# Score tiles of 64 by 32, a first batch in pieces, TensorE in source order and two earlier loads in a fused attention and WaveMLP kernel

## The chip, the cores and the metric

The kernel runs on one core of a Trainium2 chip. The metric is the device time of one execution in microseconds (us); lower is better. A time is the median of several executions, with the lowest and highest in brackets. A profile has its own span, about 2 us shorter than the device time of the same execution (172.6 us beside 174.73 us for the kernel before).

A ratio is the mean time of one kernel's fast runs over the mean time of the other's fast runs of the same rounds, with a 95% interval. It is therefore not quite the ratio of the medians that are quoted.

## The reference

```python
# B=4 batches, H=8 heads, S=768 tokens, D=64; window 96, 8 global keys
scores = q @ k.T / sqrt(64) - slope[h] * dist        # masked to window + global keys
x      = softmax(scores) @ v                         # -> (B, 768, 512)
theta  = x @ w_theta                                 # 512 x 512
y      = w_tok_r @ (x * cos(theta)) + w_tok_i @ (x * sin(theta))   # 768 x 768 token mixing
u      = x + y
out    = u + relu(u @ w_ch)                          # 512 x 512
```

## The kernel before

A batch passes through fixed stages: scores (TensorE), exponentials (ScalarE), values (TensorE), division into `x_sb` (VectorE), transposition to `xT`, `theta` (96 matmuls), sines (ScalarE), products `zri` (VectorE), mixing (288 matmuls of 512 columns in all four batches), `u`, `uT`, and the channel matmul `chan`. The attention of batch b+1 is woven into the mixing of batch b, so that TensorE has mixing to do while scores wait for exponentials. For batch 0 there is nothing to weave it into: its attention is a latency chain before the first mixing matmul. Batches are counted from 0.

In batch 0, and for q and k of batches 1 and 2, TensorE transposes. `xT` and `uT` of batches 1 to 3 (but for the very last token block), and q and k of batch 3, are transposed by DMA, issued one after another from SyncE (SP).

The local window needs, for each block of 128 keys, the block's own 128 queries and the next 128. Of the second half only 96 keys count, so the 8 global keys are overlaid there: VectorE makes `kG`, a copy of `kT` with global keys in it.

```python
def kglob(b, p):                      # VectorE: copy, then overlay the 8 global keys
    ...
    nc.vector.tensor_copy(out=kG, in_=kT[:, T:(NT - 1) * T].rearrange(...))
    nc.vector.tensor_copy(out=kG[:, :, 0:NG], in_=kT[:, None, 0:NG].to_broadcast(...))

def score_mms(b, p, c):               # weights 64 x 128, 128 columns, two heads on two row tiles
    ...
    for part in range(2 if jt + 1 < NT else 1):
        for hh in range(2):
            lhsT = kG[R, jt - 1, :] if part and jt else kT[R, own]
            nc.tensor.matmul(pb[:, hh, o:o + T], lhsT=lhsT, rhs=qT[R, (own, nxt)[part]], ...)

# batch 0 is written by hand inside `manual`, where engines keep source order
...
    trans_w(0, nc.scalar.copy); xtrans(0, NP - 1)
    for c in range(NT // 2):
        theta(0, c, 0); theta(0, c, 1)
manual.close()                        # from here the scheduler may reorder within an engine
```

The line numbers in the profiles are these:

| operation | before | after | e3 (before with the new tiles) |
|---|---|---|---|
| score matmuls / exponentials | L295 / L302 | L288 / L296 | L290 / L298 |
| values / `x_sb` | L352 / L362 | L343, batch 0 L363 / L349, L367 | L348 / L358 |
| theta / sines | L389 / L395 | L394 / L402 | L385 / L391 |
| mixing / chan | L409 / L434 | L425 / L450 | L405 / L430 |
| `kG` | L218, L220 | none | none |
| q,k cast `qkn` / its transposes | L229 / L244 | L223 / L238 | L224 / L239 |
| DMA transposes xT / uT / kT, qT | L366 / L423 / L262 | L377 / L439 / L255 | L362 / L419 / L257 |

The softmax here doesn't subtract the row's maximum and nothing guards it: scores larger than these inputs give would overflow.

## Time and profile before

The time before is 174.58 us (174.41 to 174.96). The page of the profile gives, per engine, busy time, share of the span and instructions, and per DMA queue its packets, megabytes and share:

```profile
span 172.6 us, 3652 instructions
PE 159.9 (93%) x1482; PEld 83.5 (48%) x1482; DVE 128.5 (74%) x288; ACT 99.1 (57%) x124; POOL 37.9 (22%) x45
...
q8 instruction: 11, 0.18, 0.4%
```

TensorE (PE) is the limit over the whole, but 93% busy does not say where the rest goes. The stage table does. I worked it out from the start times of TensorE's matmuls in the trace; "idle" is the time between starts less the work between them, at the spacing that this trace shows at full clock (216 ns for 512 columns, 56 ns for a transpose, 29 ns for a value matmul, and so on). Every matmul is charged its time at full clock, so the slowness of a cold clock is counted as idle too: in the kernel before 512 columns take 427 ns instead of 216 until 3.9 us. The work is 144.4 us.

| stage of before | from us | lasts us | of it idle us |
|---|---|---|---|
| first matmul to first theta | 1.2 | 26.8 | 11.1 |
| batch 0: theta to mixing | 28.0 | 5.2 | 0.0 |
| batch 0 mixing to batch 1 mixing | 33.16 | 47.20 | 6.3 |
| batch 1 mixing to batch 2 mixing | 80.36 | 33.90 | 3.1 |
| batch 2 mixing to batch 3 mixing | 114.26 | 33.57 | 2.7 |
| batch 3 mixing to last matmul | 147.83 | 20.82 | 0.1 |

The chain of waits (start us, duration us, what) shows the start as a chain through VectorE (DVE), with `kG` and `x_sb` in it:

```profile
7.78 1.01 DVE kG L218
8.81 0.18 DVE kG L220
...
26.33 0.56 DVE x_sb L362
...
28.15 3.45 PE pb L389 x16
31.60 1.53 PE ps L389 x7
33.16 2.84 ACT cs L395 x5
```

From 43 to 61 us VectorE is full. The busy table of that stretch (stretch, length, then PE, PEld, DVE, ACT, POOL busy with counts, PE clock, DMA, GB/s) has it at 17.94 of 18 us:

```profile
43.00:61.00 18.00, 17.20 (x228) 10.56 (x226) 17.94 (x41) 12.28 (x16) 5.74 (x7) 1.00 2.38 175
```

### The profile page before, as it was taken

What the parts mean: (1) busy time and instruction counts of PE and PEld (TensorE: products, weight loads), DVE (VectorE), ACT (ScalarE), POOL (GpSimd) and SP (SyncE); (2) the same over time, 40 slices, a digit from 0 to 9 for tenths busy, and PEclk for the clock granted to TensorE, in tenths of its full rate; (3) what the DMA queues carried; (4) which work ended last, traced back from release to release, by engine and by line L of the source; (5) the groups of instructions that cost most, each with busy time, mean ns of one, the idle gap of its engine ahead of it and who ended that gap; (6) DMA issues with size and microseconds to landing.
All of it is one profiled execution on the core that took longest, in us unless ns stands there. A gap on an engine that the chain in (4) does not pass through costs nothing.

```text
span 172.6 us, 3652 instructions
## 1 busy us (share of the span) xinstructions
PE 159.9 (93%) x1482; PEld 83.5 (48%) x1482; DVE 128.5 (74%) x288; ACT 99.1 (57%) x124; POOL 37.9 (22%) x45
## 2 busy tenths in 40 slices
PE   6479979999999999999999998999999989999991
PEld 1245655455756566544455463444554634444440
DVE  7678965678999999999587588597786837724443
ACT  2479676999497595489834740979348308500010
POOL 8974355005272010099300000000000000000000
PEclk9999999999999999999999999999999999999998
DMA  5999999999999999879999997787138571323335
GB/s 146 192 193 178 210 208 209 204 204 171 160 204 175 166 155 128 132 97 154 210 141 80 224 158 165 138 152 226 30 76 113 135 171 40 142 41 102 100 93 182
DMA packets 75088, 25.92 MB, mean 150 GB/s; under 512 B 63168, under 2 KB 72128, under 8 KB 75072
## 3 DMA queue, kind: packets, MB, share of 16 engines
q0 software_dynamic: 45680, 12.45, 78.4%
q1 hardware_dynamic: 28976, 12.72, 36.6%
q10 hardware_dynamic: 416, 0.52, 0.9%
q8 instruction: 11, 0.18, 0.4%
q14 instruction: 5, 0.04, 0.1%
HBM read 25.69 MB, written 6.29 MB: 185 GB/s over the span
## 4 chain that ended last, share of the span: by engine, by line
PE 59%; DVE 21%; ACT 10%; DMA 6%; issue 1%; SPq 0%; DVEq 0%; ACTq 0%
PE ps L409 29%; PE ps L434 10%; PE pb L389 5%; PE pb L295 4%; PE pb L352 4%; DVE x_sb L362 4%; ACT etab L142 3%; PE ps L389 3%; ACT e L302 3%; DMA qk<-in_k_dram 3%; DVE kG L218 2%; DVE e L312 2%; ACT cs L395 2%; DMA kT<-qk 2%; DMA xT<-x_sb 2%; PE ps L244 2%
## 5 line engine op out<-in xcount | busy, mean ns | idle before, releaser
L409 PE MATMUL ps<-zri,w_tokT 128*128 128x512 bf16 x288 | 70.6, 380 | 0.3 <-DVE o_sb L440 0.2
L302 ACT ACTIVATE e<-pb 128x1024 bf16<-128x1024 f32 (+1 forms) x48 | 43.6, 958 | 23.1 <-PE pb L295 22.9
L409 PEld LDWEIGHTS <-w_tokT 128*128 128x128 bf16 x288 | 26.1, 98 | 29.0 <-issue 1.0
L414 DVE TENSOR_TENSOR u<-x_sb,ps 128x512 bf16<-128x512 bf16 x24 | 16.4, 682 | 14.6 <-PE ps L409 14.6
L434 PE MATMUL ps<-w_ch_bf,uT 128*128 128x512 bf16 x96 | 24.2, 379 | 0.0
L398 DVE TENSOR_TENSOR zri<-x_sb,cs 128x512 bf16<-128x512 bf16 x48 | 17.9, 418 | 8.0 <-ACT cs L395 7.8
L440 DVE SCALAR_TENSOR_TENSOR o_sb<-ps,u 128x512 f32<-128x512 f32 (+1 forms) x25 | 16.5, 662 | 3.1 <-PE ps L434 3.1
L395 ACT ACTIVATE cs<-pb,halfpi 128x1024 bf16<-128x1024 f32 x8 | 8.9, 1116 | 15.7 <-PE pb L389 15.7
L312 DVE TENSOR_TENSOR e<-e,etab 128x1024 bf16<-128x1024 bf16 (+1 forms) x24 | 14.7, 615 | 3.4 <-ACT e L302 3.4
L389 PE MATMUL pb<-w_theta_bf,xT 128*128 128x512 bf16 x64 | 15.2, 379 | 1.0 <-DMA xT<-x_sb 1.0
L295 PE MATMUL pb<-qT,kT 64*128 64x128 bf16 x224 | 15.6, 219 | 0.6 <-DVE qT L211 0.3
L295 PEld LDWEIGHTS <-kT 64*128 64x128 bf16 x224 | 9.0, 94 | 14.1 <-issue 12.5
L389 PEld LDWEIGHTS <-xT 128*128 128x128 bf16 x96 | 9.0, 98 | 12.0 <-DMA xT<-x_sb 2.4
L428 ACT COPY uT<-ps 128x512 bf16<-128x512 bf16 x7 | 4.1, 587 | 18.6 <-PE ps L427 18.6
L352 PEld LDWEIGHTS <-e 128*128 128x128 bf16 x352 | 12.7, 97 | 3.3 <-issue 1.5
L434 PEld LDWEIGHTS <-uT 128*128 128x128 bf16 x96 | 8.9, 98 | 10.0 <-ACT uT L428 0.3
L295 PE MATMUL pb<-qT,kG 64*128 64x128 bf16 x128 | 11.7, 217 | 1.2 <-DVE kG L220 1.2
L88 POOL DMA_DIRECT2D vn<-in_v_dram x5 | 9.7, 1930 | 12.2 <-DVE vn L68 10.6
L362 DVE TENSOR_TENSOR x_sb<-pb,rec 128x768 bf16<-128x768 f32 x12 | 11.4, 949 | 0.3
L315 DVE TENSOR_TENSOR e<-e,etab 128x1024 bf16<-128x1024 bf16 x12 | 8.2, 684 | 2.8 <-ACT e L302 2.8
L352 PE MATMUL pb<-vn,e 128*128 128x65 bf16 x168 | 9.6, 193 | 0.3 <-DVE x_sb L362 0.3
L82 POOL DMA_DIRECT2D qk<-in_q_dram x8 | 7.4, 920 | 8.8 <-DVE qkn L229 5.0
(74 smaller groups left out, 203.0 us busy)
## 6 DMA issues: line engine op xcount, KB each, us to landing
out_dram<-o_sb SPq DMA_DIRECT2D x23, 256.0 KB, 2.4
vn<-in_v_dram POOLq DMA_DIRECT2D x3, 768.0 KB, 22.7
qk<-in_q_dram POOLq DMA_DIRECT2D x2, 768.0 KB, 21.0
qk<-in_k_dram POOLq DMA_DIRECT2D x2, 768.0 KB, 23.6
w_nat<-in_moe_w_tok_r_dram POOLq DMA_DIRECT2D x3, 384.0 KB, 13.7
w_nat<-in_moe_w_tok_i_dram POOLq DMA_DIRECT2D x3, 384.0 KB, 14.6
vn<-in_v_dram POOLq DMA_DIRECT2D x2, 384.0 KB, 8.9
qk<-in_q_dram POOLq DMA_DIRECT2D x8, 96.0 KB, 9.7
```

The lines of the kernel that those rows point to most:

```text
L295: nc.tensor.matmul(pb[:, hh, o:o + T], lhsT=lhsT, rhs=qT[R, (own, nxt)[part]], start=bool(b), stop=bool(b) or (jt == NT - 1 or (j == 1 and ...
L302: ins = nc.scalar.activation(e_c, pb[:, :, 0:n], AF.Exp, scale=scale).ins
L312: nc.vector.tensor_mul(e_c, e_c, tab[:, :, s0:s0 + n // T].rearrange("p a s n -> p a (s n)"))
L352: nc.tensor.matmul(o, lhsT=l_, rhs=r_, start=(i_ == 0), stop=(i_ == len(mms) - 1))
L362: nc.vector.tensor_mul(xv, po4[:, :, :, 0:D], rec.to_broadcast([T, n, NT, D]))
L389: nc.tensor.matmul(pb[j_] if last else pb[:, j_, :], lhsT=xT[:, dc, st(j_)], rhs=w_theta_bf[:, dc, :], start=(dc == 0), stop=(dc == NC - 1))
L395: nc.scalar.activation(o, p_, AF.Sin, **bias)
L398: nc.vector.tensor_mul(zri[b][:, i_, 2 * c + j_, :].rearrange("p (g d) -> p g d", g=NP), xb[:, :, 2 * c + j_, :], cs[:, i_, j_].rearrange( ...
L409: anchor["pe"] = nc.tensor.matmul(ps, lhsT=w_tokT[wi][:, st, tt * T:(tt + 1) * T], rhs=zri[b][:, wi, st, :], start=(st == 0 and wi == 0), ...
L414: anchor["dve"] = nc.vector.tensor_add(u_sb[b, tt].rearrange("p (g d) -> p g d", g=NP), x_sb[b][:, :, tt, :], ps.rearrange("p (g d) -> p g ...
L434: nc.tensor.matmul(ps_c, lhsT=uT[:, dc, :], rhs=w_ch_bf[:, dc, :], start=(dc == 0), stop=(dc == NC - 1))
L440: nc.vector.scalar_tensor_tensor(o_sb[:, cols], in0=ps_c[:, cols], scalar=0.0, in1=u[:, cols], op0=ALU.max, op1=ALU.add)
```

## The change

The intent is to shorten the start, to take `kG` off VectorE, and to save changes of tile mode. What such a change costs is in the trace of before: from a mixing matmul to the first score of a visit 311 ns pass (216 between two mixing matmuls), and from the last score to the next matmul of 512 columns 148 ns (a pair of scores takes 56), so 92 to 95 ns each way. Its parts:

1. Scores on tiles: weights of 64 x 32, mostly 256 columns, eight tiles at once. Only the first group of 32 keys needs the global keys, so a slice of `kT` serves and `kG` goes.
2. Batch 0 by pieces: values in 12 pieces, theta starting while values still run, the first two token blocks mixed in a hand-written order; warm-up matmuls 6 to 5.
3. TensorE keeps source order after batch 0 too (`ordered`).
4. q and k of batch 1 are loaded ahead of the last third of the token weights; the weaving starts earlier (0.3 to 0.1).

Smaller edits ride along: in batch 0 the first loads of q and k swap their queues, all eight `diag` tiles are made at the start, and one copy of token weights moves from ScalarE to VectorE.

```diff
+            if tt == NT - 2:                      # load_w: ahead of the last third of w_tok
+                load_all_qk(1)
-                for hh in range(2):               # score_mms
-                    lhsT = kG[R, jt - 1, :] if part and jt else kT[R, own]
-                    nc.tensor.matmul(pb[:, hh, o:o + T], lhsT=lhsT, rhs=qT[R, (own, nxt)[part]], ...)
+            for g in range(T // GS):              # GS = 32
+                parts = [(own, 0, 1), (slice(0, GS), 1, n)][:n] if g == 0 and jt else [(own, 0, n)]
+                for keys, a, z in parts:
+                    for hh in range(2):
+                        nc.tensor.matmul(pb[P, hh, (2*j+a)*T:(2*j+z)*T], lhsT=kT[R, keys],
+                                         rhs=qT[R, (jt+a)*T:(jt+z)*T], ...)
 ...
-    load_all_qk(1)
-    warm(6)
+    warm(5)
 ...
+    values0(2, 1)                                 # batch 0, the end of the hand-written order
+    values0(3, 1)
+    theta_mms(0, 0, 0)
+    xtrans0(1, dve)
+    theta_mms(0, 0, 1)
+    theta_sines(0, 0)
+    ...
+    theta_mms(0, 2, 0)
+    theta_mms(0, 2, 1)
+    theta_sines(0, 2)
+    mix(0, 0, 0)
 ...
+    ordered = ExitStack()
+    ordered.enter_context(tc.manual_schedule(engines={mybir.EngineType.PE}))
 ...
-        weave(main, side, 0.3 if b == 0 else 0.0, 0.9)
+        weave(main, side, 0.1 if b == 0 else 0.0, 0.9)
 ...
+    ordered.close()
```

## The prediction

> **What bounds it.** From 28 us to the end TensorE is the limit; the busy table gives it 93% of 172.6 us. From start-to-start times in its timeline (216 ns for 512 columns, 56 ns a transpose, 29 ns a value matmul, 28 ns a score matmul) I estimate 146 us of array work. The rest is array idle: about 12 us before 28 us, 6.5 us from 28 to 80, under 6 us after, 3.5 us of tail. The first 28 us are a latency chain: in the chain of waits VectorE is nearly unbroken from 6.8 to 25 us (kG, x_sb, qkn, qT, xT); the first mixing matmul (L409) starts at 33.2 us, held by the sines (L395), which start at 29.9. From 43 to 61 us VectorE is busy 17.9 of 18 us and ScalarE did the bias tables (L142) until 42.4, with q and k of batch 1 arriving near 41 us; the array loses 4.5 us there.
>
> **What changes.**
> 1. kG disappears: 16 copies of 0.39 us and 16 of 0.18 us, 9.1 us of VectorE; 2.4 us lie in the start chain, 4.6 us in the saturated stretch 43 to 80 us.
> 2. Scores: 352 matmuls of 64x128 weights by 128 columns become 896 of 64x32, mostly 256 columns. In the trace two row tiles start 3 to 4 ns apart and a pair takes 56 ns; [...]so eight should overlap too (the trace shows only two). Then a key block costs an estimated 110 ns against 112: no change. Entering and leaving the tile mode costs about 95 ns each way; the instruction order has 28 such visits against 38 (-1.9 us)[...]. Net near zero. [...]
> 3. First batch by pieces: values in 12 pieces, theta beginning while the last values run. ScalarE runs exponentials nearly back to back from about 9 to 23 us. I estimate the sines at 24.5 us, the first mixing at 27.5, the first two token blocks mixed near 33.5 instead of 39: 4 to 5.5 us.
> 4. q and k of batch 1 land near 32 us (two loads of token weights fewer ahead of them), so the saturated VectorE stretch begins earlier. This keeps the gain of 3 through batch 1; with kG gone it adds 1.5 us.
> 5. TensorE in source order: fewer mode changes, but no filling of waits, for example where three score visits run close together and wait for PSUM and exponentials: -1 to +1.5 us. After 80 us little changes.
>
> **Sum.** 174.6 - 5 (start) - 1.5 (VectorE stretch) + 0.5 (scores) + 0.4 (order) = 169.0 us. Range 164.5 to 174.5. Chances: faster 0.68, same 0.26, slower 0.06.
>
> **Signs.** Right: first mixing matmul at 26 to 29 us; batch 1's theta at about 67 us instead of 72; VectorE busy 7 to 9 us lower; score matmuls starting 3 to 6 ns apart, a pair of chunks lasting about 0.52 us. Wrong: score matmuls 25 ns apart or more; waits of scores for exponentials above 3 us in all; a longer time from batch 2's theta to the end.
>
> **What would break it.** [...]eight diagonals ahead of the first casts delaying the start[...]; stalls of the fixed order behind the bias tables; later token weights arriving too late for their transposes.

The sum came to 174.6 - 5 - 1.5 + 0.5 + 0.4 = 169.0 us. "Net near zero" and the +0.5 us for scores stand as my estimates. That eight tiles overlap as two do was my extrapolation from the trace of before.

## The result, and the profile after

The changed kernel takes 180.2 us (180.0 to 180.71, four runs); the kernel before took 174.77 us (174.41 to 176.08, four runs). The ratio is 1.0301 (1.0243 to 1.0359): slower by 3%. Executions over 1.5% slower than the fastest of the same kernel are left out of the means. The page after:

```profile
span 178.0 us, 4681 instructions
PE 159.0 (89%) x1996; PEld 85.4 (48%) x2025; DVE 125.3 (70%) x265; ACT 97.6 (55%) x119; POOL 37.9 (21%) x45
...
q8 instruction: 16, 0.26, 0.7%
```

There are 1,029 recorded instructions more (some matmuls have no record: 1,996 stand beside 2,025 weight loads), and queue q8, named "instruction", has moved 16 blocks of 16 KB instead of 11. The stages, worked out as before:

| stage | before us | after us | difference |
|---|---|---|---|
| first batch's mixing starts | 33.16 | 32.26 | -0.9 |
| batch 0 mixing to batch 1 mixing | 47.20 | 50.76 | +3.6 |
| batch 1 mixing to batch 3 mixing | 67.47 | 70.20 | +2.7 |
| batch 3 mixing to last matmul | 20.82 | 20.82 | 0 |

The gain at the start is 0.9 us, and two losses follow that have, as the experiments show, different causes. The start first. The chain of waits after:

```profile
25.51 1.08 PE pb L394 x5
...
27.64 0.42 DVE x_sb L367
28.19 0.43 DVE x_sb L367
28.67 0.28 PE ps L373 x2
29.01 1.03 PE pb L394 x4
30.03 0.67 PE ps L170 x12
30.70 1.73 PE pb L394 x8
32.43 0.86 PE ps L425 x4
```

`kG` is gone from the chain. In its place theta (L394) waits piece by piece for `x_sb` and the small transposes (L373). Then 12 transposes of token weights and the last 8 theta matmuls stand in the fixed order ahead of the first mixing matmul (L425). The first sines start at 26.6 us instead of 29.9, but the mixing does not start 3 us earlier, because all of theta is still ahead of it. Before the first mixing TensorE's array is idle for 10.4 us after and 11.1 us before, by the count of the stage table. These figures hide a cold clock: full clock came at 12.5 us instead of 3.9. With the matmuls ahead of it charged at the doubled time that they show (427 and 107 ns), the idle time is an estimated 6 us after and 9.7 before. So the pieces did remove waits, while cold matmuls took about 3 us more; e1 shows how much of that an earlier clock gives back.

Next, the stretch from the first mixing to batch 1's. In the chain of waits after:

```profile
48.34 0.86 PE ps L425 x4
49.20 0.39 PE pb L288 x16
49.62 3.57 ACT e L296 x4
53.23 0.37 PE pb L288 x12
...
64.21 1.73 ACT e L296 x2
```

For 3.57 us the chain runs through four exponentials on ScalarE. TensorE's timeline shows three groups of scores there, each behind a wait for an exponential, 1.32 us together:

```profile
51.61 0.41 PE L288 MATMUL pb<-qT,kT 64*32 64x256 bf16 x18 [0.54 <-ACT e L296]
52.31 0.42 PE L288 MATMUL pb<-qT,kT 64*32 64x128 bf16 x20 [0.29 <-ACT e L296]
53.23 0.37 PE L288 MATMUL pb<-qT,kT 64*32 64x128 bf16 x18 [0.49 <-ACT e L296]
```

In the kernel before the scheduler had put mixing between such groups:

```profile
51.77 0.61 PE L409 MATMUL ps<-zri,w_tokT 128*128 128x512 bf16 x2
...
52.63 0.60 PE L409 MATMUL ps<-zri,w_tokT 128*128 128x512 bf16 x2
```

The busy table of the whole stretch agrees; TensorE falls from 17.20 to 14.30 us while VectorE is still nearly full:

```profile
43.00:61.00 18.00, 14.30 (x314) 9.52 (x323) 17.43 (x31) 12.10 (x15) 6.95 (x8) 1.00 2.21 179
```

The tiles themselves work. The timeline of TensorE shows a visit of four key blocks after as one group of 38 matmuls:

```profile
83.98 0.63 PE L288 MATMUL pb<-qT,kT 64*32 64x256 bf16 x38
```

Inside it the trace has starts 3 to 4 ns apart on eight tiles (83.976, 83.980, 83.983, ...) and a new key block every 112 ns (84.096, 84.208, 84.320). So the array time of scores is what was predicted.

Last, q and k of batch 1. They land at 31.5 and 35.3 us instead of 37.4 and 41.3. VectorE's timeline shows when their first cast (L223) starts after, which is 40.77 us:

```profile
38.32 0.69 DVE L430 TENSOR_TENSOR u<-x_sb,ps 128x512 bf16<-128x512 bf16 x1 [0.95 <-PE ps L425]
39.18 0.69 DVE L430 TENSOR_TENSOR u<-x_sb,ps 128x512 bf16<-128x512 bf16 x1 [0.17 <-PE ps L425]
39.78 1.01 DVE L171 COPY w_tokT<-ps 128x768 bf16<-128x768 bf16 x2
40.77 0.43 DVE L223 COPY qkn<-qk 128x768 bf16<-128x768 bf16 x1
```

And before, which is 41.28 us:

```profile
41.28 1.16 DVE L229 COPY qkn<-qk 128x768 bf16<-128x768 bf16 x4
```

The data came 6 us earlier and the work began 0.5 us earlier. In VectorE's queue the casts stand behind `u` of token blocks 0 and 1 (38.32 and 39.18 us), which in the new order finish together and late.

### The profile page after: what moved, and what is told of

The parts are those of the page before. It is cut to its first block, busy times and chain, and to the rows that moved or that the text cites. A ratio compares the mean times of both kernels' runs of the same rounds, so it can differ in the third digit from the quotient of the medians.

```text
span 178.0 us, 4681 instructions
## 1 busy us (share of the span) xinstructions
PE 159.0 (89%) x1996; PEld 85.4 (48%) x2025; DVE 125.3 (70%) x265; ACT 97.6 (55%) x119; POOL 37.9 (21%) x45
## 4 chain that ended last, share of the span: by engine, by line
PE 72%; ACT 12%; DVE 8%; DMA 3%; issue 3%; POOL 0%; DVEq 0%; POOLq 0%
PE ps L425 31%; PE ps L450 11%; PE pb L394 7%; ACT e L296 7%; PE pb L288 6%; PE pb L343 4%; DMA xT<-x_sb 3%; PE pb L268 3%; PE ps L238 3%; PE ps L394 2%; PE ps L206 2%; ACT cs L402 1%; PE ps L170 1%; DVE x_sb L367 1%; PE ps L363 1%
## 5 line engine op out<-in xcount | busy, mean ns | idle before, releaser
L425 PE MATMUL ps<-zri,w_tokT 128*128 128x512 bf16 x269 | 65.9, 379 | 2.7 <-issue 1.3
L425 PEld LDWEIGHTS <-w_tokT 128*128 128x128 bf16 x288 | 26.3, 98 | 31.0 <-DVE w_tokT L171 1.8
L430 DVE TENSOR_TENSOR u<-x_sb,ps 128x512 bf16<-128x512 bf16 x24 | 16.4, 685 | 12.5 <-PE ps L425 12.5
L450 PE MATMUL ps<-w_ch_bf,uT 128*128 128x512 bf16 x91 | 23.3, 379 | 0.4 <-issue 0.2
L288 PE MATMUL pb<-qT,kT 64*32 64x256 bf16 (+1 forms) x896 | 17.8, 257 | 5.1 <-ACT e L296 2.3
L402 ACT ACTIVATE cs<-pb,halfpi 128x1024 bf16<-128x1024 f32 x9 | 10.0, 1115 | 20.6 <-PE pb L394 19.8
L394 PE MATMUL pb<-w_theta_bf,xT 128*128 128x512 bf16 x70 | 17.1, 379 | 2.7 <-DMA xT<-x_sb 2.6
L288 PEld LDWEIGHTS <-kT 64*32 64x32 bf16 x896 | 10.8, 92 | 17.8 <-issue 14.3
L394 PEld LDWEIGHTS <-xT 128*128 128x128 bf16 x96 | 8.8, 98 | 13.3 <-DMA xT<-x_sb 4.1
L343 PEld LDWEIGHTS <-e 128*128 128x128 bf16 x264 | 9.6, 97 | 3.3 <-issue 1.1
L245 ACT COPY kT<-ps 128x768 bf16<-128x768 bf16 x8 | 6.4, 799 | 7.9 <-PE ps L238 7.9
L402 ACT ACTIVATE cs<-pb 128x1024 bf16<-128x1024 f32 x9 | 9.2, 1022 | 0.0
```

The source lines that it names most:

```text
L288: nc.tensor.matmul(pb[P, hh, (2 * j + a) * T:(2 * j + z) * T], lhsT=kT[R, keys], rhs=qT[R, (jt + a) * T:(jt + z) * T], start=bool(b), stop ...
L343: nc.tensor.matmul(o, lhsT=l_, rhs=r_, start=(i_ == 0), stop=(i_ == len(mms) - 1))
L394: nc.tensor.matmul(pb[j_] if last else pb[:, j_, :], lhsT=xT_sb[b][:, dc, st(j_)], rhs=w_theta_bf[:, dc, :], start=(dc == 0), stop=(dc == ...
L402: nc.scalar.activation(o, p_, AF.Sin, **bias)
L425: anchor["pe"] = nc.tensor.matmul(ps, lhsT=w_tokT[wi][:, st, tt * T:(tt + 1) * T], rhs=zri[b][:, wi, st, :], start=(st == 0 and wi == 0), ...
L430: anchor["dve"] = nc.vector.tensor_add(u_sb[b, tt].rearrange("p (g d) -> p g d", g=NP), x_sb[b][:, :, tt, :], ps.rearrange("p (g d) -> p g ...
```

## The experiments

Sixteen kernels were run; all gave correct results. Times are medians; "before" is always the kernel before in the same rounds. The theory at the outset was that the fixed order causes the loss. The rivals were the tiles (by their own waits, or by the longer instruction stream), a cold clock, and the loads.

### e1: more warm-up matmuls in the changed kernel

```diff
-    warm(5)
+    warm(8)
```

> The changed kernel with 8 idle matmuls at the start instead of 5. Cold-clock theory: with 5 of them the TensorE clock was raised only at 12.5 us (before: 3.9 us with 6), and about 7 us of the start chain are TensorE pieces at half speed; with 8 the clock comes up near 4 us and the kernel gains 1.5 to 3 us (about 177.5 to 178.5 us in the chip's time), first mixing matmul near 30.5 us instead of 32.4. Rival (VectorE chain limits the start): clock comes up early, but under 0.7 us is gained, about 179.7.

Measured: 179.31 us (178.68 to 179.91), ratio to before 1.0251 (1.0187 to 1.0315). TensorE reached full clock at 5.7 us instead of 12.5, and the first mixing started at 31.29 us instead of 32.26. So a cold clock costs the changed kernel about 0.9 us; that lies between the two expectations, and the start shows the same gain (1.0 us). It was partly chance: e7 has five warm-up matmuls as well, its profile has full clock at 7.5 us, and its first mixing starts at 31.74 us. The profiles here have the change of clock at 3.9 us (before), 9.2 (e3), 9.7 (e4) and 12.5 (after). In the kernels with the old first batch it made no difference: with the change at 9 to 10 us, as at 3.9, the first mixing started at 32.9 to 33.2 us.

### e2: the changed kernel with free order

```diff
-    ordered.enter_context(tc.manual_schedule(engines={mybir.EngineType.PE}))
```

> The changed kernel, but after the first batch TensorE is again ordered by the scheduler (the one line that fixes its order is taken out). Fixed-order theory: array idle time after 33 us falls by 4 to 6 us, to about that of the kernel before; time 174.5 to 176.5. Rival (the tiles or the earlier loads make the later batches slower, whatever the order): within 1 us of 180.2.

Measured: 177.62 us (177.21 to 177.73), ratio 1.0144 (1.0097 to 1.0191). The fixed order costs 2.6 us in the changed kernel (180.2 - 177.62), less than the fixed-order theory expected and more than its rival. The gain lies where it should: batch 0 mixing to batch 1 mixing takes 48.39 us instead of 50.76, and from there to batch 3's mixing it takes 70.17 instead of 70.20. Half of the loss remains, so the order is not the only cause.

### e3: the kernel before with the new tiles alone

```diff
     def kglob(b, p):
-        ...            # the two copies
+        pass
     def score_mms(b, p, c):
-        ...            # 64 x 128 weights
+        ...            # the changed kernel's 64 x 32 tiles
```

> The kernel before with only the scores on 64 by 32 tiles and kG gone. Tile-neutral theory (a key block costs 112 ns either way, VectorE is relieved of 9 us): 171.5 to 174.5, faster by 0 to 3 us. Rival (544 more matmuls with their loads cost TensorE time): 176 or more.

Measured: 178.23 us (177.76 to 178.71), ratio 1.0183 (1.0131 to 1.0236). The tiles alone cost 3.3 us, although they take 9 us of copies off VectorE and no array time is added. Batch 0 mixing to batch 1 mixing takes 48.42 us (+1.2), and from batch 1's mixing to the last matmul 91.45 us (+3.2).

The second part shows in SyncE's timeline, which issues the DMA transposes one after another. Before:

```profile
99.56 1.65 SPq L423 DMA_TRANSPOSE uT<-u  x1
...
104.58 1.24 SPq L366 DMA_TRANSPOSE xT<-x_sb  x1
...
137.24 1.22 SPq L423 DMA_TRANSPOSE uT<-u  x1
138.55 1.24 SPq L366 DMA_TRANSPOSE xT<-x_sb  x1
```

With the tiles:

```profile
99.39 2.79 SPq L257 DMA_TRANSPOSE qT<-qk  x1
...
106.87 1.24 SPq L362 DMA_TRANSPOSE xT<-x_sb  x1
...
140.11 2.57 SPq L419 DMA_TRANSPOSE uT<-u  x1
142.77 1.24 SPq L362 DMA_TRANSPOSE xT<-x_sb  x1
```

A transpose that usually occupies SyncE for 1.2 us occupies it for 2.79 and 2.57 us, and the last `xT` of the batch stands behind it. Counted from the start of batch 2's mixing, the last `xT` of batch 3 is issued after 26.6 us (142.77 - 116.19) instead of 24.3, and theta waits for it. Of these 2.3 us the longer issue is 1.35 us (2.57 - 1.22); the `xT` before it was already 0.9 us late (138.80 - 116.19 against 135.94 - 114.27). At exactly those moments the trace has a packet on the queue "instruction": at 100.0 us (1.77 us long) and at 140.1 us (1.50 us long). So there was a new theory: fetches of TensorE's instruction stream, which come in blocks, hold up the DMA transposes, and a stream that is 1,088 entries longer has more of them.

### e4: the kernel before in fixed order

```diff
+    ordered = ExitStack()
+    ordered.enter_context(tc.manual_schedule(engines={mybir.EngineType.PE}))
     rest = []
     for b in range(B):
     ...
+    ordered.close()
```

> The kernel before with only TensorE's order fixed to the source order after the first batch. Fixed-order theory: slower by 3 to 6 us, 178 to 181, with more array idle time after 33 us, before scores that wait for exponentials and before transposes that wait for copies. Rival: within 1 us of 174.7.

Measured: 179.30 us (178.94 to 179.71), ratio 1.0245 (1.0197 to 1.0294). The order alone costs 4.4 us, and again between batch 0's and batch 1's mixing (51.19 us instead of 47.20). There the waits of TensorE that are not filled are for VectorE's copies and for exponentials, in the view of who waited for whom from 33 to 82 us:

```profile
PE ps L244 <- DVE w_tokT L169: 2.0, 2, 1.7
PE pb L352 <- ACT e L302: 1.4, 2, 0.9
```

Neither line appears in the same stretch of the kernel before. From batch 1's mixing to batch 3's the order cost 0.7 us more (68.20 against 67.47).

### e5: many no-ops in the kernel before

```diff
                     start=(st == 0 and wi == 0), stop=(st == NT - 1 and wi == 1)).ins
+                with tc.issue_after(anchor["pe"]):
+                    for _ in range(4):
+                        nc.tensor.nop(hint="keep", nofuse=True)
```

> The kernel before with four no-operations behind each of the 288 mixing matmuls on TensorE's queue: 1152 instructions more, about as many as the small tiles add (1088), no other order changed on any engine. Instruction-fetch theory (each 16 KB fetch of TensorE's instructions holds up a DMA transpose by about 1 us): 15 or 16 fetches instead of 11, 5 or more transposes issued over 1.45 us instead of 3, theta of the later batches waits longer for xT, time longer by 0.7 to 2.5 us. Rival (the tiles lose by themselves): within 0.5 us of the kernel before, with mixing matmuls still 216 ns apart in both cases.

Measured: 186.53 us (185.69 to 186.72), ratio 1.0663 (1.0628 to 1.0698). The run is inconclusive and outside both expectations. The number of fetches rose to 16 as intended, but the no-ops also delayed the matmuls themselves: the spacing of mixing matmuls has a median of 218 ns, but a quarter is at 303 ns or more. In the view of who waited for whom this wait has grown to 31.4 us, where the page of before has 1.0 us for it:

```profile
PEld L409 <- issue: 31.4, 130, 1.4
```

### e6: the earlier load of q and k alone

```diff
+            if tt == NT - 2:
+                load_all_qk(1)
 ...
     load_w()
-    load_all_qk(1)
```

> The kernel before with only q and k of batch 1 loaded ahead of the last third of the token weights. The prediction's step 4: VectorE's saturated stretch begins earlier, gain of 1 to 3 us. Rival (the scheduler keeps its compiled order and TensorE has mixing to do until then, so an earlier arrival ends no wait): within 0.7 us.

Measured: 175.33 us (174.62 to 175.91), ratio 1.0042 (1.0003 to 1.0082). The earlier load gains nothing by itself: q and k landed at 31.5 and 35.3 us, as in the changed kernel, and VectorE's first cast of them started at 41.08 us (before: 41.28). Its stage times agree with those of before within 0.2 us.

### e7: shorter score visits in fixed order

```diff
-            steps.append((1800, lambda i_=i_: [scores(b, *pc) for pc in chunks[i_:i_ + 2]]))
+            for pc in chunks[i_:i_ + 2]:
+                add(900, scores, b, *pc)
```

> The changed kernel with one score chunk at a visit in place of two, TensorE's order still fixed: TensorE has mixing between one chunk and the next. Fixed-order theory (scores stand in TensorE's queue waiting for exponentials to free PSUM): waits inside score visits fall by 2 us or more, time 177.5 to 179[...]. Rival: within 0.7 us of 180.2.

Measured: 180.46 us (179.38 to 181.22), ratio 1.032 (1.0264 to 1.0376). The waits inside score visits from the first mixing to batch 1's fell from 3.41 to 1.61 us, yet nothing was gained in total: that stretch got 0.5 us shorter (50.22 us), and the later batches got 0.75 us longer. The waits named in the chain were real but not the lever; which waits took their place was not traced.

### e8: the new first batch with the old tiles afterwards

The kernel has the changed kernel's batch 0 (with its tiles, 8 warm-up matmuls and the earlier load), free order, and for batches 1 to 3 the old scores with `kG`.

```diff
-    warm(5)
+    warm(8)
-    ordered.enter_context(tc.manual_schedule(engines={mybir.EngineType.PE}))
+    # score_mms0 (tiles) in batch 0; score_mms and kglob of the kernel before in batches 1 to 3
```

> The first batch of the changed kernel (by pieces, on small tiles, 8 idle matmuls, early q and k), and batches 1 to 3 as before: 64 by 128 tiles with kG, TensorE ordered by the scheduler. If the loss of the change lies in the fixed order and in the small tiles of batches 1 to 3, the 1.9 us by which the first mixing started earlier in the run with 8 idle matmuls remain: 172 to 174, faster than before by 1 to 2.5 us. Rival (the first batch by pieces costs something later, in the way the batches overlap): 174.5 or more.

Measured: 176.36 us (174.94 to 177.15), ratio 1.0081 (1.0026 to 1.0136). Batch 2's mixing to batch 3's takes 33.58 us, as before (33.57), so without tiles in the later batches that loss is gone. But the start's gain (31.46 against 33.16 us) is lost by batch 1's mixing (81.63 against 80.36). The third of batch 1's four `xT` (the expectation of e11 calls it the last) took 5.41 us to land, across a fetch at 69.2 us, and theta idled 2.41 us. ("Theta idled", here and below, is the array's idle time from the last mixing matmul of one batch to the first of the next.) The kernel before has much the same slow transpose, 5.05 us, across a fetch at 70.7 us; there theta came 1.9 us later and did not have to wait for it.

### e9 and e10: tiles with the fetches moved by no-ops

e9 is e3 with one no-op behind each of batch 0's 72 mixing matmuls, and e10 has two. With 4,054 entries in TensorE's stream and 16 fetches, e3 has on average a fetch to about 253 entries.

```diff
+                if b == 0:
+                    with tc.issue_after(anchor["pe"]):
+                        for _ in range(1):          # e10: 2
+                            nc.tensor.nop(hint="keep", nofuse=True)
```

> The kernel before with small tiles and no kG (178.2 us in its own run), with one no-operation behind each of the 72 mixing matmuls of batch 0: no other order changes on any engine, TensorE's later instruction fetches come 72 instructions earlier. Instruction-fetch theory: other transposes than before are the slow ones, those that overlap no fetch land within 3.6 us, and the waits of theta for xT in batches 2 and 3 (3.8 us lost there in the run without padding) change by 0.7 us or more in all, and the time with them. Rival (the small tiles delay xT by the work itself): the same two transposes late by as much, time within 0.5 us of 178.2.

> The same with two no-operations each, 144 instructions: over half the distance between two fetches. Same theories; if a padding moves the fetches of about 100 and 140 us off the end of the mixing phases, 176 to 177.5 us; if it moves others onto them, 178 to 179.

Measured: e9 179.52 us (178.33 to 181.72), ratio 1.0232 (1.0172 to 1.0292); e10 180.29 us (179.35 to 182.01), ratio 1.031 (1.0237 to 1.0382). Batch 1's mixing to the last matmul falls from 91.45 us (e3) to 89.58 and 89.05 us; before has 88.29. Theta's waits for DMA transposes from 80 to 157 us (total us, times, longest) show it, first before:

```profile
PE pb L389 <- DMA xT<-x_sb: 1.0, 2, 0.5
```

then e3:

```profile
PE pb L385 <- DMA xT<-x_sb: 3.1, 4, 1.2
```

and e10:

```profile
PE pb L385 <- DMA xT<-x_sb: 1.0, 2, 0.5
```

So moving the fetches gave back 2.4 of the 3.2 us that the tiles cost there. But the no-ops lengthened batch 0's mixing stage (40.3 us in e3, 41.8 and 46.0 here; in e10's profiled run a drop of the granted clock from 67 to 74 us, to a mean of 0.981 over the run, added to it), so the total did not improve, and the proof was not clean.

### e11 and e12: the mixed kernel with the fetches moved by no-ops

```diff
+                if b == 0 and tt > 1:
+                    with tc.issue_after(anchor["pe"]):
+                        for _ in range(2):          # e12: 3
+                            nc.tensor.nop(hint="keep", nofuse=True)
```

> The hybrid (176.4 us) with two no-operations behind each of the 48 mixing matmuls of batch 0 after the first two token blocks, 96 instructions. In the hybrid the last xT of batch 1 took 5.4 us to land across a fetch at 69 us and theta of batch 1 lost 2.4 us. Instruction-fetch theory: with the fetch elsewhere that transpose lands in about 3 us and the kernel gains 1 to 2.5 us, 174 to 175.5. Rival: within 0.5 us of 176.4.

> The same with three no-operations each, 144 instructions. Same theories; gain of 1 to 2.5 us where no fetch falls on the last xT of batch 1, otherwise about 176.4.

Measured: e11 176.36 us (176.11 to 178.69), ratio 1.0116 (1.0032 to 1.0201); e12 176.16 us (175.85 to 176.32), ratio 1.006 (1.002 to 1.0101). The idle time in batch 1's theta fell from 2.41 (e8) to 1.77 and 0.89 us. In e12 a fetch then came at 102.3 us, on an `xT` of batch 2, whose theta now idled 2.04 us. The wait moved rather than went, and both totals are within the rival's 0.5 us of e8.

### e13: no tiles, the fetches moved, all orders kept

The 76 no-ops lie in gaps of batch 0 in which TensorE waits anyway. The order of all instructions on every engine is the same as before; I compared the two programs, and the two traces have the same order on every engine.

```diff
+    idle(20)                                   # idle(n): n no-ops on TensorE
     warm(6)
+    idle(24)
 ...
+            idle(8)                            # three times, and once before trans_w(0)
             xtrans(0, p - 1, ...)
```

> The kernel before, with 76 no-ops on TensorE in the first batch's idle gaps (around the warm-up matmuls and ahead of four groups of transposes). The order on every other engine and of every matmul is unchanged. All later instruction fetches come 76 instructions earlier; from the trace of before I place them at about 88, 95, 111, 127 and 136 us. The one at 95 falls into the close row of SyncE transposes before batch 2's theta, the one at 136 on the second-last transpose of batch 3's. Fetch theory: first mixing of batch 1 to the last matmul grows from 88.3 to 89.3 to 90.3 us with no tiles at all, total +1 to +2 us. Rival (fetches do not matter, only the tiles' own waits do): 88.3 us and the total within 0.5 us.

Measured: 176.95 us (176.03 to 177.38), ratio 1.01 (1.0058 to 1.0142). Batch 1's mixing to the last matmul took 89.70 us instead of 88.29: the fetch theory's range, and not the rival's. Batch 0's mixing to batch 1's is nearly unchanged (47.49, before 47.20 us). The fetches came at 83.2, 94.1, 108.8, 126.6 and 136.9 us; 88, 95, 111, 127 and 136 were expected. The one at 94.1 us did not do what was expected of it: the `xT` that it met landed after 2.85 us, and theta itself waited no longer for its `xT`. The loss came from two others. The one at 136.9 us lies on the second-last transpose of batch 3. SyncE's timeline has it at 1.68 us, and the last `xT` at 139.94 instead of 138.55 us (before, shown with e3):

```profile
136.85 1.68 SPq L370 DMA_TRANSPOSE xT<-x_sb  x1
...
139.94 1.24 SPq L370 DMA_TRANSPOSE xT<-x_sb  x1
```

The one at 108.8 us lies on a `kT`. Its copy to `kG` stands in VectorE's queue ahead of products that the mixing of batch 2 needs. VectorE's timeline before:

```profile
110.63 0.30 DVE L218 COPY kG<-kT 128x512 bf16<-128x512 bf16 x1 [0.69 <-DMA kT<-qk]
```

and in e13:

```profile
111.55 0.29 DVE L222 COPY kG<-kT 128x512 bf16<-128x512 bf16 x1 [1.66 <-DMA kT<-qk]
```

That `kT` landed 2.75 us after its issue before, and 3.74 us after it here. Batch 2's mixing starts 0.9 us later. Nothing but 76 empty instructions in idle time was changed, so the place of the fetches is shown as a cause, of 1.4 us here. This rests on one profile of each kernel, but e6, whose fetches after 80 us lie within 0.6 us of those of before, repeats the stage to 0.04 us (88.33). The total is 1% slower; its interval is clear of 1.

### e14: tiles, the fetches moved, all orders kept

The edit is that of e13, applied to e3.

> The kernel of e3 (tiles alone) with the same 76 no-ops in the idle gaps of the first batch, so without the no-ops between mixing matmuls that made e9 and e10 slow before batch 1. Fetches expected at about 99, 117, 123, 132 and 137 us: the one that lay on the second-last transpose of batch 3 (140) moves into a gap, the one at 100 stays in the close row. Fetch theory: array lost in batch 3's theta falls from 2.0 to about 0.7 us, first mixing of batch 1 to the last matmul from 91.45 to 89.8 to 90.4 us, total 176.7 to 177.5 us. Rival (e9's gain came from the no-ops between matmuls): no change, 178.2 us.

Measured: 178.13 us (177.45 to 179.34), ratio 1.0187 (1.0126 to 1.0247). Batch 3's theta idles 0.68 us instead of 2.04, as expected. But a fetch at 105.5 us now falls between two transposes of batch 2, whose theta idles 2.47 us instead of 1.72. Batch 1's mixing to the last matmul takes 90.84 us, 0.6 less than e3, where 1.05 to 1.65 less was expected; the total is the one that the rival expected. The mechanism is confirmed in the one theta; as a repair it failed.

The runs with tiles also show a loss that moving fetches does not touch. From batch 2's mixing to batch 3's e9, e10 and e14 all take 34.5 us, 0.9 us more than before (33.56), though theta idles no longer there. In e14 most of it lies at two entries into score visits, 0.76 and 0.61 us from the last mixing matmul to the first score instead of 0.31, where the scores wait for an exponential. So for this part the rival named at the outset, the tiles' own waits, holds. Whether they come from the tiles or from the other order in which the scheduler then places the score visits no run separates.

### e15: the mixed kernel, fetches moved

The no-ops are placed as in e13, applied to e8.

> The kernel of e8 (first batch by pieces, tiles only there, free order) with 76 no-ops in the first batch's idle gaps. Fetch expected at 65.5 instead of 69.2 us, so before the last two transposes of batch 1 (issued at 67 and 70). Fetch theory: the last of them lands in about 3 us instead of 5.4, the array loses under 1.2 us in batch 1's theta instead of 2.4, total 175.0 to 175.8 us. Rival (loads alone lengthen those transposes): 2 us or more lost, 176.4 us.

Measured: 177.31 us (177.06 to 179.14), ratio 1.015 (1.0092 to 1.0209); the profile fell on the slowest of the four. The fetch came at 69.6 us, not at 65.5, partly because the first mixing itself began later (32.94 us; e8: 31.46), so these no-ops were not free. Batch 1's theta idled 0.84 us all the same, but batch 2's theta idled 2.49 us. Only 0.67 us of that is theta's wait for `xT`; the rest stands between theta and the mixing, where VectorE waited 2.1 us for a `kT` that landed after 4.18 us, across a fetch at 112.0 us, much as in e13. The total is a miss for both theories.

### e16: the three repairs on the changed kernel together

Free order, 8 warm-up matmuls and the 76 no-ops.

> The changed kernel with free order, 8 warm-up matmuls and 76 no-ops in the first batch's gaps: the three repairs together. If they add: 177.6 (free order) - 0.9 (clock) - 0.5 to 1.5 (fetches moved off the transposes) = 175.2 to 176.2 us. If the repairs only move the waits: 177 us or more.

Measured: 178.62 us (177.93 to 180.01), ratio 1.0213 (1.0153 to 1.0273). The repairs do not add up: batch 3's theta idles 0.69 us, batch 2's 2.28 us, and batch 0's mixing stage 9.45 us. None of the sixteen beats the kernel before.

### What the runs together say of fetches and transposes

From the trace I took, for each DMA transpose issued after 92 us, the time from issue to landing, and whether an instruction fetch (of q8) fell into it or began at most 1.3 us before. Those issued earlier are left out: in before and after they took 2.8 to 8.7 us while loads of q, k and v were still landing, and every one of them met a fetch as well, so the two cannot be told apart there.

| kernel | fetch: transposes, median us (longest) | no fetch: transposes, median us (longest) |
|---|---|---|
| before | 6, 4.02 (4.57) | 24, 2.73 (3.54) |
| after | 9, 3.85 (5.20) | 22, 2.60 (3.00) |
| e3 | 8, 4.09 (4.66) | 22, 2.60 (3.62) |
| e13 | 9, 3.30 (4.41) | 21, 2.54 (2.82) |

A second queue named "instruction", q14, moves four or five blocks of 8 KB and is left out. With it counted as well, the longest of "no fetch" falls to 2.79 us in e3 and 2.78 us after; in before it stays at 3.54. The table alone shows that the two go together; that one causes the other is shown by e13.

TensorE's stream has 2,966 entries before and 4,054 in e3, and the traces have 11 and 16 fetches of 16 KB: on average one to about 270 and 253 entries. In e5 nothing but no-ops in TensorE's queue took the fetches from 11 to 16, so these are fetches of TensorE's instructions. TensorE itself need not wait for one: around the fetches of before at 99.2 and 142.3 us no two of its starts are more than 216 ns apart. A transpose under way is lengthened all the same (in e13 a median of 3.30 us with a fetch, 2.54 without). How the two get in each other's way no run here shows.

## Why the prediction was wrong

It said 169.0 us, with 6% for slower; it is 180.2 us. The sum had five terms. Those of the order and of the tiles were measured in runs on different kernels (order on the changed kernel, tiles on the kernel before), so they need not add, and that they nearly do is partly chance:

| term | predicted us | measured us | from |
|---|---|---|---|
| start (steps 1, 3) | -5 | -0.9 | first mixing 33.16 to 32.26 |
| VectorE stretch (steps 1, 4) | -1.5 | 0 | e6 (step 4 alone; step 1 gained nothing in e3 either) |
| scores on tiles (step 2) | +0.5 | +3.3 | e3 |
| order (step 5) | +0.4 | +2.6 | e2 (+4.4 in e4) |
| sum | -5.6 | +5.0 | total measured: +5.4 |

**Step 1, `kG`: right in size, without effect.** It costs 9.1 us of VectorE and is gone. Summed by lines, VectorE's records fell by about 7 us: batch 0's smaller pieces of `x_sb` and `rec` took 1.2 us more, a token-weight copy moved over from ScalarE 0.6, the `xT` pieces 0.5. The busy figure of the page, which counts overlapping records once, fell by 3.2 us. The sign "7 to 9 us lower" fails on the page. The step that failed is that this time was worth anything: with the tiles alone (e3) VectorE has the same relief, and the stretch before batch 1's mixing is 1.2 us longer.

**Step 2, tiles: the mechanism was right, the sum was not.** Starts 3 to 4 ns apart, a key block per 112 ns, a pair of chunks 0.52 to 0.56 us: all as predicted; the extrapolation from two tiles to eight held. A longer way out of a visit, which the forecast had set against the fewer visits, hardly came: from the last score of a visit to the next mixing or channel matmul the median is 148 ns before and 160 ns in e14. "Net near zero" failed. I counted array time and mode changes and did not count instructions. The tiles lengthen TensorE's stream by 1,088 entries and add five fetches. From batch 1's mixing on they cost 3.2 us in e3, of which 2.4 us vanish when the fetches fall elsewhere (e10); e13 produces 1.4 us of the same kind without tiles. The rest is the tile kernels' own waits (0.9 us in one stage, see e14).

**Step 3, first batch by pieces: the largest error.** Sines at 24.5 us were predicted and came at 26.6; the first mixing at 27.5 came at 32.3. Two things were missed. Theta's pieces wait for VectorE's pieces, one after another, until 28.6 us; the last exponential ends at 24.1 us, 1.2 us earlier than before, and that limits the gain. And an early sine does not start the mixing while the remaining theta and the weight transposes stand ahead of it in a fixed order. A late clock took 0.9 us more (e1).

What was won at the start did not last either. In none of the runs with the new first batch did batch 1's mixing start before 80.6 us (e2), against 80.36 in the kernel before, although the first mixing started up to 1.9 us earlier. Between 43 and 61 us VectorE is busy for 17.8 to 17.9 of 18 us in e2, e8 and e12 as it is in the kernel before. That this is what holds batch 1 back is likely and not shown by a run of its own.

**Step 4, q and k: they landed when predicted and were not used.** The step took the load for the limit. VectorE's queue was (cast at 40.8 against 41.3 us), and e6 shows no gain.

**Step 5, order: the mechanism was named, the size was wrong.** It allowed for -1 to +1.5 us, and named "no filling of waits, for example where three score visits run close together"; that is what the chain shows. The cost was 2.6 us (4.4 us in e4). "After 80 us little changes" holds for the order in the changed kernel (70.17 against 70.20 us; in e4 it cost 0.7 us) and fails for the change as a whole, by step 2.

**The list of signs did its work.** Of the signs named for "wrong", one appeared in part: the page after has TensorE idle for 5.1 us ahead of score matmuls, against 1.8 us before (0.6 and 1.2 in the two score groups), but puts only 2.3 of it on exponentials. Another appeared in full: a longer time from batch 2's theta to the end (65.75 against 63.26 us). Batch 1's theta in its main group began at 74.9 us, not 67 (before 72.2). The chance of 6% for slower was too small above all because each term with a gain was taken at nearly its full size.

**What stays open.** Why e3's stretch before batch 1's mixing is 1.2 us longer is not settled; the array idles 1.3 us inside score visits there, but e9 and e10 disturbed just this stretch. The kernel before may owe some of its speed to where its fetches happen to fall: e13 shows that one other placement is 1% slower (176.95 against 174.91 us), but not how good the best is.

## What to carry to other kernels

Splitting matmuls so that the array takes the same time was not free here (e3: +3.3 us): count the instructions, find in the trace where the instruction fetches fall, and look whether a DMA transpose on the critical path shares that moment (in e13 the place of the fetches alone cost 1.4 us). Fix the order of an engine only where it is better than what a scheduler finds; where several engines feed each other, a fixed order can turn a late input into idle time (2.6 us in e2, 4.4 in e4), and removing one wait may gain nothing (e7). An earlier load or an earlier sine is worth only as much as the first instruction that can use it moves, so look at what stands before that instruction in its engine's order.
